# A fused attention and gated-unit kernel: output-row copies set apart, a later reciprocal, a third buffer for projected keys and queries

## The chip, the cores and the metric

The kernel runs on one core of one Trainium2 chip. The metric is the device time of one execution in microseconds (us); 814.01 us is the median of three runs of the kernel before (813.37 to 815.41). The profile is of one more execution, which took 813.36 us.

Names used below: PE is the matrix engine (TensorE), DVE the vector engine (VectorE), ACT the scalar engine (ScalarE), POOL is GpSimd. SP (SyncE) computes nothing here; it issues the DMAs, one after the other, in the order of the program. A DMA whose data is not there yet makes SP stand still, and every DMA behind it waits too.

## The reference

The input is x, 2048 rows of 640. It is normalised, goes through a 32-head attention (20 columns a head) and through a gated unit of width 1728, and the two results are multiplied and added to x:

```python
    def _A_ref(x, wqkv, wo):
        ...
        scores = jnp.einsum("bhqd,bhkd->bhqk", q, k) * scale
        p = _softmax(scores, axis=-1)
        o = jnp.einsum("bhqk,bhkd->bhqd", p, v)
        return (lambda x, *d: x.transpose(*d))(o, 0, 2, 1, 3).reshape(B, S, D) @ wo
    def _B_ref(x, w_gate, w_up, w_down):
        ...
        h = _sigmoid(g) * u
        return jnp.einsum("bsf,fd->bsd", h, w_down)
    xn = _layernorm(x, axis=-1)
    s = _A_ref(xn, A_wqkv, A_wo)
    g = _silu(_B_ref(xn, B_w_gate, B_w_up, B_w_down))
    return x + s * g
```

## The kernel before

**Blocks.** The attention is cut into 32 blocks (`NBLK`): eight groups of four heads times four chunks of 512 queries. Blocks 0 to 23 are six groups one after the other; in blocks 24 to 31 the last two groups alternate chunk by chunk (`gc_of`). A block has 64 jobs (`NJOB`): 16 tiles of 128 keys for each of its four heads. A job is a score matmul (line 883), an exponential, and a matmul with the values into the accumulator `oacc` (line 920). `oacc` holds 20 output rows and one row of sums for each of the four heads.

**Two ways to an exponential.** Most jobs go to ACT (line 82; two jobs of 512 columns in one instruction, `pt`, or one at a time, `px`). The others go to DVE: each score tile is converted to 16-bit integers (`iv`, line 1264), and then, for four jobs at a time, three passes (lines 998, 1001, 1004) make two halves of the exponential, which PE adds up by two matmuls.

**An order made at build time.** From line 1172 on the program steps through a clock of its own (`now`, in us) with a cost for each instruction, and writes PE's, ACT's and DVE's instructions in the order in which this clock lets them start. The engines then run these fixed orders and wait for each other through semaphores. Between attention work PE is given "items" (the projections, the gated unit, the output projection), chosen by position and by whether their inputs are due in the planner's clock. DMAs stand in SP's queue in the order in which the planner calls them.

**Normalising a block.** When the last value matmul of a block is out, `norm_a` copies `oacc` on DVE (`on`, line 949) and issues two DMAs: the rows of sums go to memory (`ld`, line 951) and come back spread over 128 partitions (`lt`, line 953). The pair `(time, block, on, lt)` is put in the list `timed`. Once that time has come, DVE runs `norm_b`: the reciprocal (`rt`, line 959), a DMA to memory (`rd`, line 961), four DMAs that bring it back broadcast to 32 rows each (`rl`, line 964); and four POOL products, each of 128 columns (`on_bf`, line 969), are put in `pool_q`, due 7.2 later. They leave `pool_q` in one of two ways:

- `beat` (line 933), after a DVE instruction that reads PSUM, emits one due product and makes it wait for the DVE instruction before that one, so that it runs beside the PSUM read;
- `flush("n")`, which `norm_a` and `norm_b` of the next block call first, emits whatever is left, with no such tie.

With the last product `norm_c` is called, which issues the copies of the block's 80 output rows to their place in `oU` (line 988): four or five DMAs, since a head whose rows cross a multiple of 128 takes two. `o_at[b]` says when the planner takes these rows as landed; the output projection of four row tiles (`mk_out`, line 778) waits for `o_at` of blocks 25, 27 and 29 (`need=ALT + 1 + 2 * (tt // 4)`). Block 31, the last, is normalised in another way, by transposes (`chain`, from line 1055), and the last four row tiles are projected at the end (`early`, `late_mm`, `tail_steps`). Block 30 is the last that goes through `norm_a` to `norm_c`.

**Projected keys and queries.** For the heads from 8 on, keys and queries are projected six heads at a time (`mk_ku`, `mk_qu`, line 536). DVE copies each 120 x 512 result out of PSUM into a tile with the tag `ku` (lines 547 and 586), SP writes it to memory (lines 548 and 587), and it is loaded later in the layout of the blocks (`kT`, `q`; lines 630 to 639). The rows of bounds (`bt`, line 606) take a tile of the same tag. There are two such tiles, so a copy waits until the DMA from the tile two before has been read out.

Of the kernel before, what the change touches and what calls it, by code (L numbers as in the profile page):

```python
# [11 lines left out]
BF16 = mybir.dt.bfloat16  # L12
# [6 lines left out]
P = 128  # L19
# [5 lines left out]
QC = 512  # L25
# [3 lines left out]
UC = UH * DH  # L29
# [22 lines left out]
def kernel(  # L52
# [11 lines left out]
    nc = tc.nc  # L64
# [27 lines left out]
    wk = ctx.enter_context(tc.tile_pool(name="wk", bufs=2))  # L92
# [8 lines left out]
    oU = persist.tile([P, KD, S], BF16, name="oU")  # L101
# [32 lines left out]
    def load_wv(pr):  # L134
        w = wk.tile([P, KD, 2 * GC], BF16, tag="wv", bufs=1, name="wv")
        nc.sync.dma_start(out=w, in_=wqkv_v[:, :, 2, pr * 2 * GC:(pr + 1) * 2 * GC])
        return w
# [306 lines left out]
    EL, PL = 0.15, 0.21  # L444
    T_F, T_PV, T_MM, T_MODE = 0.2133, 0.2133, 0.2133, 0.107
    T_IV, T_ON = 0.605, 0.60
    T_PASS = (0.1333, 0.1333, 0.27)

    def t_exp(n):
# [5 lines left out]
    def gc_of(b):  # L455
        if b < ALT:
            return divmod(b, NQC)
        return NG - 2 + (b - ALT) % 2, (b - ALT) // 2
# [80 lines left out]
    def mk_ku(u, c, at):  # L539
        st = {}  # L540

        def alloc():
            st["ps"] = misc_ps()

        def ev():
            st["k"] = wk.tile([P, QC], BF16, tag="ku", bufs=2, name="ku")[0:UC, :]
            ins = nc.vector.tensor_copy(out=st["k"], in_=st["ps"][0:UC, :])
            nc.sync.dma_start(out=kD[u][:, c * QC:(c + 1) * QC], in_=st["k"])
            return ins

        def mx():
            if u not in mku:
                mku[u] = [wk.tile([UC, NQC], FP32, tag="mk4", bufs=2, name="mk4"), 0, None]
            ins = nc.vector.tensor_reduce(out=mku[u][0][:, c:c + 1], in_=st["k"], axis=AXISX, op=ALU.max,
                                          apply_absolute_value=True)
            mku[u][1] += 1
            if mku[u][1] == NQC:
                mk = wk.tile([UC, 1], FP32, tag="mk", bufs=2, name="mk")
                nc.vector.tensor_reduce(out=mk, in_=mku[u][0], axis=AXISX, op=ALU.max)
                mku[u][2] = wk.tile([UC, UH], BF16, tag="mdu", bufs=2, name="mdu")  # L560
                ins = nc.vector.tensor_scalar_mul(out=mku[u][2], in0=esum_u[0:UC, :], scalar1=mk[:, 0:1])
            return ins

        def end(t):
            if mku[u][1] == NQC:
                ev_at[("mdu", u)] = t + 0.3
        return Item([("PE", alloc, [(T_MM, lambda kd=kd: u_mm(st, u, 1, c, kd)) for kd in range(KD)]),
                     ("DVE", 0.60, ev, "free", mark("kD", u, c)), ("DVE", 0.60, mx, "", end)], at,
                    pre=[("wu", u)])

    aqs = {}

    def mk_qu(u, c, at):
        st = {}

        def alloc():
            st["ps"] = misc_ps()

        def ab():
            aqs[(u, c)] = wk.tile([P, QC], BF16, tag="aq", bufs=4, name="aq")  # L580
            return nc.vector.tensor_scalar(out=aqs[(u, c)][0:UC, :].bitcast(I16), in0=st["q"].bitcast(I16), scalar1=0x7FFF,
                                           scalar2=0, op0=ALU.bitwise_and, op1=ALU.bitwise_or)

        def ev():
            st["q"] = wk.tile([P, QC], BF16, tag="ku", bufs=2, name="qu")[0:UC, :]
            ins = nc.vector.tensor_scalar_mul(out=st["q"], in0=st["ps"][0:UC, :], scalar1=qscale)  # L586
            nc.sync.dma_start(out=qD[u][:, c * QC:(c + 1) * QC], in_=st["q"])
            return ins
        return Item([("PE", alloc, [(T_MM, lambda kd=kd: u_mm(st, u, 0, c, kd)) for kd in range(KD)]),
                     ("DVE", 0.60, ev, "free", mark("qD", u, c)),  # L590
                     ("DVE", 0.19, ab, "", mark("aq", u, c))], at, pre=[("bD", u - 1)] if u else [])

    def mk_bu(u, at):
        st = {}

        def alloc():
            st["ps"] = misc_ps()

        def mm():
            for c in range(NQC):  # L600
                nc.tensor.matmul(st["ps"][32 * c:32 * c + UH, :], lhsT=mku[u][2], rhs=aqs[(u, c)][0:UC, :],
                                 start=True, stop=True, tile_position=(0, 32 * c), skip_group_check=True)

        def ev():
            bt = wk.tile([P, QC], BF16, tag="ku", bufs=2, name="bt")
            ins = nc.vector.tensor_copy(out=bt, in_=st["ps"])
            for c in range(NQC):
                nc.sync.dma_start(out=bD[u][:, c * QC:(c + 1) * QC], in_=bt[32 * c:32 * c + UH, :])
            return ins
        return Item([("PE", alloc, [(T_MM + 2 * T_MODE, mm)]),  # L610
                     ("DVE", 0.60, ev, "free", mark("bD", u))], at,
                    pre=[("mdu", u)] + [("aq", u, c) for c in range(NQC)])
# [333 lines left out]
    def norm_a(b):  # L946
        flush("n")
        on = w2.tile([P, QC], FP32, tag="on", bufs=2, name="on")
        beat(nc.vector.tensor_copy(out=on, in_=oacc))  # L949
        ld = dram.tile([GH, QC], FP32, name="ld", tag="ld")  # L950
        nc.sync.dma_start(out=ld, in_=on.rearrange("(j r) q -> j r q", r=32)[:, 0, :])
        lt = w2.tile([P, GH * QC // P], FP32, tag="lt", bufs=2, name="lt")
        nc.sync.dma_start(out=lt, in_=ld.rearrange("j (i c) -> (j i) c", c=GH * QC // P))
        return on, lt

    def norm_b(b, on, lt):
        flush("n")
        rt = w2.tile([P, GH * QC // P], FP32, tag="rt", bufs=2, name="rt")
        beat(nc.vector.reciprocal(out=rt, in_=lt), False)
        rd = dram.tile([GH, QC], FP32, name="rd", tag="rd")  # L960
        nc.sync.dma_start(out=rd.rearrange("j (i c) -> (j i) c", c=GH * QC // P), in_=rt)
        rl = w2.tile([P, QC], FP32, tag="rl", bufs=1, name="rl")
        for j in range(GH):
            nc.sync.dma_start(out=rl[32 * j:32 * j + 32, :], in_=rd[j:j + 1, :].broadcast_to((32, QC)))
        on_bf = w2.tile([P, QC], BF16, tag="on_bf", bufs=2, name="on_bf")

        def part(i):
            cs = slice(i * P, (i + 1) * P)
            ins = nc.gpsimd.tensor_tensor(out=on_bf[:, cs], in0=on[:, cs], in1=rl[:, cs], op=ALU.mult)  # L969
            if i == QC // P - 1:  # L970
                norm_c(b, on_bf)
                o_at[b] = now + 4.8
            return ins
        for i in range(QC // P):
            pool_q.append((now + 7.2, "n", lambda i=i: part(i)))

    def norm_c(b, on_bf):
        g, c = gc_of(b)
        for j in range(GH):
            f = g * GC + j * DH  # L980
            r = 32 * j + 1
            left = DH
            while left:
                t, o = divmod(f, P)
                m = min(left, P - o)
                if t == KD - 1:
                    o = f - FL if f >= FL else f - FK + D - FL
                nc.sync.dma_start(out=oU[o:o + m, t, c * QC:(c + 1) * QC], in_=on_bf[r:r + m, :])  # L988
                f += m
                r += m  # L990
                left -= m


    def passes(d, k):
# [109 lines left out]
    with tc.manual_schedule(engines={ENG.PE, ENG.Activation, ENG.DVE, ENG.Pool}):  # L1104
# [68 lines left out]
        while len(chain_end) < len(chain) or fill or items or glu_items or any(it.i < len(it.ops) for it in active):  # L1173
# [3 lines left out]
            if bb > blk_loaded:  # L1177
                blk_loaded = bb
                g, c = gc_of(bb)
                if c == 0 and g + 1 < PG:  # L1180
                    spread_wst(g + 1, load_wst(g + 1))
                if c == 0 and g + 1 < NG:
                    if g % 2 == 1:
                        wvs[(g + 1) // 2] = load_wv((g + 1) // 2)
            if not tail and all(ev_at.get(("h", NQC - 1, kf), 1e9) <= now for kf in range(NFT)):
                tail_load()
            active = [it for it in active if it.i < len(it.ops)]
# [18 lines left out]
            for eng in ("ACT", "DVE"):  # L1206
# [6 lines left out]
                if eng == "DVE" and norm_pending is not None and norm_pending[1] <= now and norm_pending[0] < NBLK - 1:  # L1213
                    free["DVE"] = now + T_ON
                    oacc_at[0] = now + T_ON + EL
                    timed.append((free["DVE"] + 6.5, norm_pending[0]) + norm_a(norm_pending[0]))
                    norm_pending = None
                    continue
                it = next((e for e in active if e.i < len(e.ops) and e.ops[e.i][0] == eng and e.open(now)), None)
# [5 lines left out]
                if eng == "ACT":  # L1225
# [24 lines left out]
                            s["ends"] = max(s["ends"], end + EL)  # L1250
                            nexp += 1
                    continue
                tm = next((x for x in timed if x[0] <= now), None)
                if tm is not None:
                    timed.remove(tm)
                    norm_b(*tm[1:])
# [173 lines left out]
            now += STEP  # L1430
        assert not items and not glu_items and not any(it.i < len(it.ops) for it in active)
        for tm in timed:
            norm_b(*tm[1:])
        flush("n", "o")
        tail_steps()

# [28 lines left out]
```

## Time and profile before

| | |
|---|---|
| median of three runs | 814.01 us (813.37 to 815.41) |
| profiled execution | 813.36 us |
| its span, first to last instruction | 811.6 us |
| granted TensorE clock | 0.995 |
| ACT: exponentials of two jobs (`pt`) | 697 of 1146 ns |
| DVE: `iv` / the three passes | 504 of 681 ns / 126 each of 685, 690 and 1221 ns |
| DVE: copy of `oacc` (949) / reciprocal (959) | 31 of 682 ns / 31 of 245 ns |
| POOL: product `on_bf` (969) | 124, median 456 ns, longest 1547 ns |
| SP: copies to `oU` (988) | 140, median 712 ns each to issue |

A line of a timeline has the start in us, the length in us, the engine and line, the operation, the tile written and read, and how often; in brackets stands the idle time of the engine before it and what ended that. The letter q behind an engine marks its instruction queue. A line of the waits has who waited, for whom, the total in us, how often, and the longest. DVE and ACT instructions overlap their neighbours a little, so that a row of `iv` starts every 0.60 us though one lasts 0.68.

### The profile page before, as it was taken

What the parts mean: (1) busy time and instruction counts of PE and PEld (TensorE: products, weight loads), DVE (VectorE), ACT (ScalarE), POOL (GpSimd) and SP (SyncE); (2) the same over time, 40 slices, a digit from 0 to 9 for tenths busy, and PEclk for the clock granted to TensorE, in tenths of its full rate; (3) what the DMA queues carried; (4) which work ended last, traced back from release to release, by engine and by line L of the source; (5) the groups of instructions that cost most, each with busy time, mean ns of one, the idle gap of its engine ahead of it and who ended that gap; (6) DMA issues with size and microseconds to landing.
All of it is one profiled execution on the core that took longest, in us unless ns stands there. A gap on an engine that the chain in (4) does not pass through costs nothing. (4 is left out here: it accounts for less than half of the span.)

```text
span 811.6 us, 17415 instructions
## 1 busy us (share of the span) xinstructions
PE 776.3 (96%) x6480; PEld 273.2 (34%) x6480; DVE 774.6 (95%) x1248; ACT 780.8 (96%) x991; POOL 107.7 (13%) x225
## 2 busy tenths in 40 slices
PE   7899999999999999999999999999999999999995
PEld 5522222333333323333333222333333223333332
DVE  7799999999999999999999999999999999999995
ACT  8899999999999999999999999999999999999991
POOL 7200000000010000000000000000100203203124
PEclk9999999999999999999999999999999999999998
DMA  5531211123222223212112131232222232312211
GB/s 160 156 103 50 66 52 40 59 58 96 63 70 69 68 58 85 66 55 61 55 58 67 51 100 54 71 104 81 63 70 60 72 88 67 123 57 82 83 52 61
DMA packets 91797, 59.96 MB, mean 74 GB/s; under 512 B 34868, under 2 KB 85604, under 8 KB 91712
## 3 DMA queue, kind: packets, MB, share of 16 engines
q1 hardware_dynamic: 91424, 58.52, 25.8%
q8 instruction: 51, 0.84, 0.4%
q14 instruction: 34, 0.28, 0.1%
q10 hardware_dynamic: 288, 0.33, 0.1%
HBM read 45.18 MB, written 11.09 MB: 69 GB/s over the span
## 5 line engine op out<-in xcount | busy, mean ns | idle before, releaser
L82 ACT ACTIVATE pt<-scA 128x1024 bf16<-128x1024 f32 x704 | 694.7, 1142 | 4.1 <-PE bk L883 3.1
L1264 DVE TENSOR_SCALAR iv<-bk 128x512 int16<-128x512 f32 x504 | 333.6, 681 | 10.2 <-PE bk L883 9.0
L883 PE MATMUL scA<-q,kT 32*128 32x512 bf16 x1401 | 273.1, 382 | 12.9 <-ACT pt L82 7.7
L883 PE MATMUL bk<-q,kT 32*128 32x512 bf16 x647 | 207.4, 383 | 0.1
L920 PE MATMUL oacc<-pt,v 128*21 128x512 bf16 x1401 | 179.4, 382 | 0.6 <-DVE on L949 0.6
L883 PEld LDWEIGHTS <-kT 32*128 32x128 bf16 x2048 | 84.1, 91 | 260.5 <-issue 249.6
L920 PE MATMUL oacc<-pb,v 128*21 128x512 bf16 x1008 | 159.7, 382 | 0.8 <-DVE pb L1004 0.7
L1004 DVE TENSOR_TENSOR pb<-iv,pb 128x2048 bf16<-128x2048 bf16 x126 | 153.9, 1221 | 1.0
L677 PE MATMUL bk<-xnT,wgu 128*128 128x512 bf16 x520 | 148.0, 383 | 1.6 <-DVE iv L1264 0.7
L969 POOL TENSOR_TENSOR on_bf<-on,rl 128x128 bf16<-128x128 f32 x124 | 59.3, 481 | 636.2 <-DVE pb L1004 160.1
L82 ACT ACTIVATE px<-bk 128x512 bf16<-128x512 f32 x143 | 100.5, 717 | 2.7 <-POOL hT L1113 1.6
L998 DVE TENSOR_SCALAR pb<-iv 128x2048 int16<-128x2048 int16 x126 | 86.3, 685 | 0.9
L1001 DVE TENSOR_SCALAR pb<-iv 128x2048 int16<-128x2048 int16 x126 | 86.9, 690 | 0.1
L723 PE MATMUL bk<-wd,hT 128*128 128x320 bf16 x448 | 83.8, 302 | 2.2 <-DVE iv L1264 1.4
L920 PEld LDWEIGHTS <-v 128*21 128x21 bf16 x2552 | 49.4, 91 | 86.4 <-issue 63.5
L677 PEld LDWEIGHTS <-wgu 128*128 128x128 bf16 x520 | 38.2, 97 | 67.6 <-issue 47.9
L920 PE MATMUL oacc<-px,v 128*21 128x512 bf16 x143 | 49.0, 382 | 0.0
L723 PEld LDWEIGHTS <-hT 128*128 128x128 bf16 x448 | 34.6, 97 | 41.4 <-issue 33.8
L536 PE MATMUL bk<-xnT,wu 128*128 128x512 bf16 x160 | 47.3, 383 | 1.2 <-DVE qu L586 1.0
L82 ACT ACTIVATE tnh<-bk 128x512 bf16<-128x512 f32 (+1 forms) x56 | 39.7, 709 | 0.1
L685 DVE SCALAR_TENSOR_TENSOR hT<-tnh,bk 128x512 bf16<-128x512 bf16 x52 | 35.3, 679 | 1.4 <-PE bk L677 0.7
L794 POOL TENSOR_TENSOR xnT<-otmp,xnT 128x160 bf16<-128x160 f32 x48 | 26.2, 567 | 47.9 <-DVE pb L1001 15.6
(111 smaller groups left out, 408.2 us busy)
## 6 DMA issues: line engine op xcount, KB each, us to landing
rl<-rd SPq DMA_DIRECT2D x124, 64.0 KB
wgu<-in_B_w_gate_dram SPq DMA_DIRECT2D x24, 320.0 KB
wgu<-in_B_w_up_dram SPq DMA_DIRECT2D x24, 320.0 KB
gq_dram<-gqs SPq DMA_DIRECT2D x24, 160.0 KB
xnT<-gq_dram SPq DMA_DIRECT2D x12, 320.0 KB
xt<-in_A_x_dram SPq DMA_DIRECT2D x16, 160.0 KB
xnT<-in_A_x_dram SPq DMA_DIRECT2D x16, 160.0 KB
out_dram<-xnT SPq DMA_DIRECT2D x14, 160.0 KB
```

What stands on the lines that cost most here:

```text
L82: return nc.scalar.add_instruction(mybir.InstActivation(func=func, name=nc.get_next_instruction_name(), engine=ENG.Activation, ins=[nc.sca ...
L536: nc.tensor.matmul(st["ps"], lhsT=wus[u][:, kd, i, :], rhs=xnT[:, c, kd, :], start=(kd == 0), stop=(kd == KD - 1))
L677: nc.tensor.matmul(st[key][0:fs, :], lhsT=w[:, i, kd, ko * P:ko * P + fs], rhs=xnT[:, c, kd, :], start=(kd == 0), stop=(kd == KD - 1))
L685: return nc.vector.scalar_tensor_tensor(out=hT[0:fs, kf, :], in0=st["t"][0:fs, :], scalar=1.0, in1=st["u"][0:fs, :], op0=ALU.add, op1=ALU. ...
L723: nc.tensor.matmul(st["ps"][:, 0:HD], lhsT=hT[:, kf, t4 * P:(t4 + 1) * P], rhs=wd[:, kf, h * HD:(h + 1) * HD], start=(kf == 0), stop=(kf = ...
L883: nc.tensor.matmul(dst, lhsT=kTs[gc_of(b)[0] % 2][32 * j:32 * j + 32, kt * P:(kt + 1) * P], rhs=qts[b % 3][32 * j:32 * j + 32, :], start=T ...
L920: nc.tensor.matmul(oacc[32 * j:32 * j + DH + 1, :], lhsT=lhsT, rhs=u["src"], start=first, stop=last, tile_position=(0, 32 * j), skip_group ...
L969: ins = nc.gpsimd.tensor_tensor(out=on_bf[:, cs], in0=on[:, cs], in1=rl[:, cs], op=ALU.mult)
L998: ins = nc.vector.tensor_scalar(out=pb[:, 0, :, :].bitcast(I16), in0=iv, scalar1=0x7F80, scalar2=1, op0=ALU.bitwise_and, op1=ALU.bitwise_or)
L1001: ins = nc.vector.tensor_scalar(out=pb[:, 1, :, :].bitcast(I16), in0=iv, scalar1=0x007F, scalar2=0x3F00, op0=ALU.bitwise_and, op1=ALU.bitw ...
L1004: ins = nc.vector.tensor_tensor(out=pb[:, 1, :, :], in0=iv.bitcast(BF16), in1=pb[:, 1, :, :], op=ALU.mult)
L1264: beat(nc.vector.tensor_scalar(out=d["iv"][:, j, :], in0=bank[bk], scalar1=B_OFF, scalar2=0.0, op0=ALU.add, op1=ALU.max))
```

## The change

Four things are changed:

- `norm_c` no longer issues a block's four or five `oU` copies in one go. For blocks 0 to 29 it puts them in `timed`, the first at once, the next each `T_OU` = 1.5 later; the main loop issues them as their time comes. `o_at[b]` grows by 1.5 for each copy after the first. Block 30 keeps the old way.
- The time after which DVE may run `norm_b` behind the copy of `oacc` is `T_LT` = 9.0 in place of 6.5, for blocks 0 to 29.
- The tag `ku` has three tiles in place of two.
- `timed` now holds two kinds of entries, told apart by their length; what is left of it at the end is run.

```diff
+    T_LT, T_OU = 9.0, 1.5
...
-            st["k"] = wk.tile([P, QC], BF16, tag="ku", bufs=2, name="ku")[0:UC, :]
+            st["k"] = wk.tile([P, QC], BF16, tag="ku", bufs=3, name="ku")[0:UC, :]
...
-            st["q"] = wk.tile([P, QC], BF16, tag="ku", bufs=2, name="qu")[0:UC, :]
+            st["q"] = wk.tile([P, QC], BF16, tag="ku", bufs=3, name="qu")[0:UC, :]
...
-            bt = wk.tile([P, QC], BF16, tag="ku", bufs=2, name="bt")
+            bt = wk.tile([P, QC], BF16, tag="ku", bufs=3, name="bt")
...
                 norm_c(b, on_bf)
-                o_at[b] = now + 4.8
...
     def norm_c(b, on_bf):
         g, c = gc_of(b)
+        parts = []
...
-                nc.sync.dma_start(out=oU[o:o + m, t, c * QC:(c + 1) * QC], in_=on_bf[r:r + m, :])
+                parts.append((oU[o:o + m, t, c * QC:(c + 1) * QC], on_bf[r:r + m, :]))
...
+        for i, (o, x) in enumerate(parts):
+            if b < NBLK - 2:
+                timed.append((now + T_OU * i, lambda o=o, x=x: nc.sync.dma_start(out=o, in_=x)))
+            else:
+                nc.sync.dma_start(out=o, in_=x)
+        o_at[b] = now + 4.8 + (T_OU * (len(parts) - 1) if b < NBLK - 2 else 0.0)
...
+            for tm in [x for x in timed if x[0] <= now and len(x) == 2]:
+                timed.remove(tm)
+                tm[1]()
...
-                    timed.append((free["DVE"] + 6.5, norm_pending[0]) + norm_a(norm_pending[0]))
+                    timed.append((free["DVE"] + (T_LT if norm_pending[0] < NBLK - 2 else 6.5), norm_pending[0]) + norm_a(norm_pending[0]))
...
-                tm = next((x for x in timed if x[0] <= now), None)
+                tm = next((x for x in timed if x[0] <= now and len(x) > 2), None)
...
         for tm in timed:
-            norm_b(*tm[1:])
+            tm[1]()
```

## The prediction

> **What bounds the kernel now.** I read first the busy times of the stretch from 31 to 793 us, the attention proper, then who waited in it, then the time line around each wait that the change touches, and last the end.
>
> ```profile
> 31.00:793.00 762.00, 742.90 (x6198) 250.84 (x6201) 741.54 (x1166) 756.74 (x941) 80.36 (x161) 1.00 0.26 73
> ACT pt L82 <- PE bk L883: 3.1, 7, 0.7
> ACT px L82 <- PE bk L883: 0.7, 1, 0.7
> DVE iv L1264 <- PE bk L883: 9.0, 18, 1.1
> DVE rt L959 <- DMA lt<-ld: 3.3, 4, 1.2
> DVE qu L586 <- DMA qD<-qu: 1.0, 1, 1.0
> ```
>
> The first line is one window: its length, then busy us of PE, weight loads, DVE, ACT and POOL, clock, DMA share and GB/s. ACT is busy 756.74 of 762.00 us: 5.3 us idle are the most that a better order at the same division of jobs could win here. DVE idles 20.5 us. The change aims at two DVE waits, 3.3 us in four places before the reciprocal and 1.0 us before one copy of queries. What ends them shows at the longest:
>
> ```profile
> 706.08 3.84 SPq L988 DMA_DIRECT2D oU<-on_bf  x5
> 709.97 0.53 SPq L951 DMA_DIRECT2D ld<-on  x1
> 710.60 2.08 SPq L1017 DMA_DIRECT2D xnT<-in_A_x_dram  x4
> 712.80 0.36 SPq L953 DMA_DIRECT2D lt<-ld  x1
> 714.99 0.25 DVE L959 RECIPROCAL rt<-lt 128x16 f32<-128x16 f32 x1 [1.23 <-DMA lt<-ld]
> 718.16 2.85 ACT L82 ACTIVATE pt<-scA 128x1024 bf16<-128x1024 f32 x3 [0.74 <-PE bk L883]
> ```
>
> The accumulator's copy starts at 706.03 and ends at 706.71, but SP is in the five `oU` copies of the block before until 709.92; the sums leave 3.3 us late, come back after DVE has arrived, and the hole of 1.23 us reaches ACT 3 us later as 0.74. The same picture, 3.0 to 3.8 us of `oU` copies ahead of `ld`, stands at the other three: holes of 0.74, 0.89 and 0.42 us on DVE at 235.73, 330.75 and 638.75, and on ACT 0.51 at 239.26, 0.42 at 336.07 and none. So 3.28 us of DVE's became **1.67 us of ACT's**. The wait of the queries at 444.72 has the same head (439.05, 3.53 us of copies, `qD` behind them at 442.68): 1.04 us on DVE, then on PE, then **0.74 us on ACT** at 446.48.
>
> **The change part by part.** No instruction is added or removed: 140 copies, 31 reciprocals, 124 products stay. Only orders move.
>
> *The copies.* Where the next block's `norm_a` flushes the last product, `norm_c` now only puts the copies on the list, and the loop finds them after `norm_a` has issued `ld` and `lt`. Elsewhere they stand 1.5 apart, so that `ld` meets one copy (0.71 us median), not 3.0 to 3.8. SP still stands at the first copy until POOL is done (58.2 us in 26 such waits, the longest 8.4), but no longer ahead of `ld` in the flushed blocks. Issue time on SP is the same in total, 140 x 0.71 = 99 us of 811.6, so nothing is lost there.
>
> *The reciprocal.* It now starts 2.5 later: 7.5 us (median of the 31) after the copy of `oacc` becomes about 10.1, the latest return seen is 8.95 (706.03 to 714.99). All four waits should go even without the copies' spreading. With it move one `rd` (0.34 us on SP), four `rl` (0.41 each) and four products. SP stands at `rd` until the reciprocal is there (65.7 us in 27, the longest 5.1); what queues behind it are loads of weights, keys and queries. PE's weight loads lost 0.4 us to `kT` in this stretch and nothing to `q`, so moving that stop costs nothing; if a load behind it became late, 5.1 us is the bound, once.
>
> *The third tile.* The copy at 444.72 would find a free tile. No instruction more. Either this or the spreading removes the 1.04.
>
> Gain on ACT: 1.67 + 0.74 = **2.4 us**. The upper bound is DVE's own 3.28 + 1.04 = 4.3, if DVE's time comes back whole; the lower is 0, if PE or the division of jobs eats it. I take 2.4, because ACT's row is the nearest to full.
>
> *What is late next, first: products.* In the 30 distances between accumulator copies (16.95 to 32.20 us, median 24), the four products now run from 15 to about 19 us after the copy. Added 2.5 by the planner's clock is 2.65 by the trace's (0.6 + 6.5 = 7.1 planned took 7.54). With each product moved so, 17 of them, in eight blocks, fall behind the next copy and are flushed without the tie to a PSUM read; today 3 do. An untied product can fall beside a DVE pass. What that costs is seen near the end, where POOL runs untied additions:
>
> ```profile
> 783.97 1.38 POOL L794 TENSOR_TENSOR xnT<-otmp,xnT 128x160 bf16<-128x160 f32 x3 [0.66 <-DVE rt L959]
> 784.88 1.01 DVE L1001 TENSOR_SCALAR pb<-iv 128x2048 int16<-128x2048 int16 x1
> ```
>
> The pass takes 1.01 where 0.68 is usual: 0.33 lost. Bounds: 0 (the product waits instead; one was stretched to 1.55) and 17 x 0.33 = 5.6 us of DVE. DVE's holes reached ACT at (1.67 + 0.74) / (3.28 + 1.04) = 0.56. I take a quarter of the products hitting a pass at its worst time: 4 x 0.33 x 0.56 = **0.7 us**. The Trainium skill speaks against this part: its page "SBUF — State Buffer", section "Who interferes with whom", says that GpSimd and DVE share a pair of ports under an exclusive lock, and that whoever starts first holds it for a whole instruction. The stretched pass above and the stretched product agree in kind; by that rule a pass could lose a whole product, and the sum would be the rival below.
>
> *Second: the output projection.* `o_at` of blocks 25, 27 and 29, four copies each, rises by 3 x 1.5 = 4.5 and by the later products. Before, the last product of block 29 runs at 774.48 and the first projection that needs it at 779.67, which is o_at's 4.8 in the trace's time: this is a real gate. After, the product is flushed at block 30's copy, 20.3 us after block 29's, near 776.0, and the gate opens (4.8 + 4.5) x 1.06 = 9.9 us later, near 786: 6.3 us late. For blocks 25 and 27 the gated unit's items fill the gap. For block 29 nothing is left (line 723 is last seen at 773.3):
>
> ```profile
> 776.86 0.39 PE L883 MATMUL scA<-q,kT 32*128 32x512 bf16 x2 [0.52 <-ACT pt L82]
> 779.18 0.39 PE L883 MATMUL scA<-q,kT 32*128 32x512 bf16 x2 [0.52 <-ACT pt L82]
> 779.67 0.84 PE L778 MATMUL bk<-wo,oU 128*128 128x320 bf16 x5
> 796.54 0.30 PE L778 MATMUL bk<-wo,oU 128*128 128x320 bf16 x1
> 798.54 0.39 PE L1025 MATMUL bk<-wo,oU 128*128 128x512 bf16 x1 [1.05 <-DMA oU<-on_bf]
> ```
>
> Without items PE idles: 0.36 (before 775.94) and twice 0.52, 1.4 us of the 3.7 from 775.94 to 779.67. In 6.3 us more that is 6.3 x 1.4 / 3.7 = 2.4 us of PE, to be paid back after the scores end at 793.5, where the chain to the end runs through PE. There, 1.05 us (798.54) and 0.68 (796.26) of PE's waits can take some of it. Bounds: 0, and the whole 6.3 us. I take 2.4 - 1.7 = **0.7 us**.
>
> The sum: -2.4 + 0.7 + 0.7 = -1.0 us. On the profiled execution's own 813.36 us (811.6 of span and 1.8 around it) that makes 812.4; the median stands 0.65 above that run, so I forecast **813.0 us** against 814.01. I take 0.3%, 2.4 us, as what a measurement here can tell from no change: under 811.6 is faster, over 816.5 slower.
>
> **The rivals.**
>
> *More comes back (faster).* DVE's 4.3 us come back whole and nothing is late: 814.0 - 4.3 = 809.7. And the planner deals the jobs anew, since each shifted reciprocal changes what it finds ready. A set of four more on DVE takes 4 x 573 ns = 2.3 us from ACT, for 4 x 0.60 + 2.6 = 5.0 us of DVE, which has that much: 807.4. Against it: ACT's idle of 5.3 caps the first way.
>
> *The last projection (slower).* Place: between block 29's products and the tail. If PE gives the eight projections no more room than now (779.67 to 796.84), they end 6.3 us later, and the 1.7 us of waits take nothing because they hang on block 30's copies: 814.0 - 2.4 + 6.3 = 817.9; with half the 2.4 us of gain, 819. It decides once the first projection comes more than the 2.4 us gained too late, after 782 (784 if the two waits do take their 1.7).
>
> *Products beside passes (slower).* All 17 at 0.33: 5.6 x 0.56 = 3.1, and 814.0 - 2.4 + 3.1 + 0.7 = 815.4; at a product's own 0.46 us, 17 x 0.46 x 0.56 = 4.4, so 816.7. For: eight short blocks. Against: a flushed product often ran free (the part may fall beside a PSUM read by chance). This is what the lock of the Trainium skill's page named above would do.
>
> *It does little.* If the later reciprocal alone had cured all, the copies' spreading would be idle; the time is the same as forecast, so no case of its own.
>
> **How the numbers follow.** Forecast, around 813.0 (811 to 815): 0.40, of which 0.06 falls under 811.6. More comes back: 0.34, all faster. Last projection: 0.16, slower. Products: 0.10, half of it slower. A new dealing of four jobs to ACT instead of DVE adds 2.3 us to any of these and takes 0.05 of the forecast's share to slower. That gives faster 0.40, the same 0.34, slower 0.26. The range must reach into both sides: down to 807.5 (the faster rival with one set), up to 818.0 (the projection's price); beyond are left 0.07 below and 0.1 above. The forecast's own range is 811 to 815.
>
> **What would show it.** Right: no wait of the reciprocal on `lt`, none of line 586 on `qD`; `oU` copies one at a time, with `ld` after at most one; ACT's idle from 31 us to the last exponential near 3 us; the first projection of the last group near 786. Wrong: the count of DVE jobs (504) moved by eight or more; new DVE waits on PE of over 3 us beyond the 9.0; passes above 0.9 us in more than ten places; or the stretch after the last exponential, 18 us now, changed by more than 2.

## The result, and the profile after

| | before | after |
|---|---|---|
| median of seven runs each (us) | 814.01 (812.82 to 816.15) | 811.31 (811.02 to 812.0) |
| profiled execution / its span | 813.36 / 811.6 | 811.31 / 809.3 |
| first exponential starts at | 30.30 | 29.97 |
| last exponential ends at | 793.50 | 789.15 |
| ACT idle between these two | 5.26 | 1.77 |
| from there to the end of the span | 18.15 | 20.19 |
| last projection of row tiles 8 to 11, behind the last exponential | 3.3 | 6.2 |

The ratio after to before is 0.9962, with a 95% interval of 0.9949 to 0.9975: faster by 0.38%; the medians lie 2.7 us apart. (Here and below the ratio is taken over all the runs, so it can differ by up to 0.1% from that of the two medians.) The runs also lie closer together, over 1.0 us in place of 3.3.

The stretch of the attention, one window of the kernel after (length, then busy us of PE, weight loads, DVE, ACT and POOL, clock, DMA share, GB/s):

```profile
31.00:789.00 758.00, 732.36 (x6115) 248.76 (x6178) 737.86 (x1159) 756.23 (x939) 78.58 (x157) 1.00 0.26 73
```

ACT now idles 1.8 of 758.00 us. Who waited there, in the kernel after (us in total, how often, the longest):

```profile
ACT pt L82 <- PE oacc L921: 0.9, 1, 0.9
ACT pt L82 <- PE bk L884: 0.2, 1, 0.2
DVE iv L1274 <- PE bk L884: 13.7, 25, 1.2
```

The rows `rt` on `lt` and line 587 (586 before) on `qD` are gone, and of ACT's eight waits on `bk` (3.8 us) one of 0.2 is left. What DVE lost there is in part lost elsewhere: its own wait for PE's scores, which stops nobody, grew from 9.0 to 13.7. DVE has 502 conversions in place of 504, and the same 126 of each pass (one of them now over half the columns): the division of jobs is as it was, give or take one pair.

But the copies do not stand as the change's spacing says. SP's part of the timeline of the kernel after, at the first block's copies and at a flushed block:

```profile
79.48 3.09 SPq L995 DMA_DIRECT2D oU<-on_bf  x4
...
560.88 2.34 SPq L995 DMA_DIRECT2D oU<-on_bf  x3
563.32 0.54 SPq L952 DMA_DIRECT2D ld<-on  x1
```

The first block's four go out back to back in 3.09 us (3.08 before). At 560.88 three copies still stand ahead of `ld`. Over the 31 blocks `ld` starts more than 2 us after the start of the copy of `oacc` in 14, against 10 before.

The end, in the timeline of the kernel after (PE, ACT, PE, DVE, PE, in order of time):

```profile
780.30 0.85 PE L779 MATMUL bk<-wo,oU 128*128 128x320 bf16 x5
...
786.08 3.08 ACT L82 ACTIVATE pt<-scA 128x1024 bf16<-128x1024 f32 x3
...
794.82 0.57 PE L779 MATMUL bk<-wo,oU 128*128 128x320 bf16 x3
...
796.11 0.32 DVE L754 TENSOR_TENSOR onq<-scA,rq 128x160 bf16<-128x160 f32 x1 [0.28 <-PE tp L1057]
...
796.80 0.39 PE L1032 MATMUL bk<-wo,oU 128*128 128x512 bf16 x1 [0.52 <-DMA oU<-on_bf]
```

The projections that need block 29 start at 780.30, 8.9 us before the last exponential ends; before it was 779.67 and 13.8 us. They end at 795.39, among the last block's own steps (`onq`, and the matmuls of line 1032).

### The profile page after: what moved, and what is told of

The parts are those of the page before. It is cut to its first block, busy times and chain, and to the rows that moved or that the text cites. A ratio compares the mean times of both kernels' runs of the same rounds, so it can differ in the third digit from the quotient of the medians.

```text
span 809.3 us, 17335 instructions
## 1 busy us (share of the span) xinstructions
PE 768.4 (95%) x6409; PEld 272.3 (34%) x6478; DVE 774.2 (96%) x1246; ACT 780.2 (96%) x989; POOL 109.1 (13%) x225
## 5 line engine op out<-in xcount | busy, mean ns | idle before, releaser
L1274 DVE TENSOR_SCALAR iv<-bk 128x512 int16<-128x512 f32 x502 | 333.0, 679 | 15.2 <-PE bk L884 13.7
L884 PE MATMUL bk<-q,kT 32*128 32x512 bf16 x642 | 201.1, 383 | 0.1
L678 PE MATMUL bk<-xnT,wgu 128*128 128x512 bf16 x476 | 141.8, 383 | 3.5 <-issue 1.3
L970 POOL TENSOR_TENSOR on_bf<-on,rl 128x128 bf16<-128x128 f32 x124 | 57.6, 471 | 629.0 <-DVE pb L1011 186.5
L537 PE MATMUL bk<-xnT,wu 128*128 128x512 bf16 x147 | 45.2, 383 | 1.4 <-issue 0.8
L795 POOL TENSOR_TENSOR xnT<-otmp,xnT 128x160 bf16<-128x160 f32 x48 | 29.9, 642 | 50.8 <-issue 28.0
```

What stands on the lines that cost most here:

```text
L537: nc.tensor.matmul(st["ps"], lhsT=wus[u][:, kd, i, :], rhs=xnT[:, c, kd, :], start=(kd == 0), stop=(kd == KD - 1))
L678: nc.tensor.matmul(st[key][0:fs, :], lhsT=w[:, i, kd, ko * P:ko * P + fs], rhs=xnT[:, c, kd, :], start=(kd == 0), stop=(kd == KD - 1))
L884: nc.tensor.matmul(dst, lhsT=kTs[gc_of(b)[0] % 2][32 * j:32 * j + 32, kt * P:(kt + 1) * P], rhs=qts[b % 3][32 * j:32 * j + 32, :], start=T ...
L1274: beat(nc.vector.tensor_scalar(out=d["iv"][:, j, :], in0=bank[bk], scalar1=B_OFF, scalar2=0.0, op0=ALU.add, op1=ALU.max))
```

## The experiments

The theory (A) was that the three kinds of wait are what the change wins. The rival (B) was that the new delays make the planner deal and order the jobs anew, and that this sets the time, for better or worse. So some kernels below keep PE's, ACT's and POOL's instructions in the order of before and move only DMAs or the reciprocal; others change the planner's numbers and let it deal. Kernels of one table were timed together.

| kernel | median (us) | ratio to before, 95% |
|---|---|---|
| before, with these | 814.25 | |
| `ku3_alone` | 813.35 | 0.9995, 0.9982 to 1.0007 |
| `copies_after_ld` | 811.46 | 0.9961, 0.9948 to 0.9974 |
| `recip_only` | 817.91 | 1.0037, 1.0022 to 1.0052 |
| `late_recip_alone` | 812.50 | 0.9977, 0.9966 to 0.9988 |

### The third tile alone

```diff
# ku3_alone, against before; in three places
-tag="ku", bufs=2
+tag="ku", bufs=3
```

> Only the third tile for projected keys and queries; every engine's order and SP's order are those of before. Theory A (removed waits come back as ACT's idle time): the 1.04 us wait of DVE at line 586 goes, ACT's idle from its first exponential to its last falls from 5.3 to about 4.5 us, and the time by 0.7 us (0.1%). Theory B (the gain is the planner's new dealing of the work): under 0.3 us, since no order changes.

The wait at the copy of queries is gone, ACT's idle is 4.75 us against 5.26, and the time is the same within its interval. The 0.74 us of ACT that the prediction put on this wait is of that size, and too small to time.

### The copies behind `ld`, orders of the engines kept

```diff
# copies_after_ld, against before
+    HOLD_OU = 2.0
...
-                nc.sync.dma_start(out=oU[...], in_=on_bf[r:r + m, :])
+                parts.append((oU[...], on_bf[r:r + m, :]))
...
+        for o, x in parts:
+            if b < NBLK - 2:
+                timed.append((now + HOLD_OU, lambda o=o, x=x: nc.sync.dma_start(out=o, in_=x)))
```

The main loop issues these entries as it does after the change; `o_at` stays. Only SP's order differs from before.

> Before with each block's oU copies issued 2.0 planner us later, all together; o_at as before, so PE, ACT, DVE and POOL keep their order and only SP's changes. Theory A with the copies' place as the cause: ld stands ahead of the copies in the flushed blocks, the four waits of the reciprocal (3.3 us) and the one of line 586 shrink to under 1 us in all, and the time falls by 1.5 to 2.4 us. Rival C (SP has no clock; where nothing flushes, the copies still come back to back ahead of ld): two or more of the four waits stay, and ld starts 2 us or more late in about as many blocks as before (11).

In the medians it wins as much as the whole change, 2.8 us. ACT's idle is 3.77 us, the wait at the copy of queries is gone, and of the reciprocal's four waits (3.28 us) three are left, 1.94 us in all. Why these are left shows in SP's part of its timeline, around the one that was longest before:

```profile
705.45 2.33 SPq L996 DMA_DIRECT2D oU<-on_bf  x3
707.89 0.52 SPq L952 DMA_DIRECT2D ld<-on  x1
708.46 1.51 SPq L996 DMA_DIRECT2D oU<-on_bf  x2
...
711.38 0.33 SPq L954 DMA_DIRECT2D lt<-ld  x1
```

Three copies still stand ahead of `ld` and two between `ld` and `lt`, so the wait fell from 1.23 us to 0.50 and did not go. At the other two that are left, three and four copies stand ahead of `ld`. Only around 325 us do all four stand behind it, and there the reciprocal's wait of 0.89 us is gone. So the signs of rival C came: three of the four waits stay, and `ld` starts more than 2 us after the start of the copy of `oacc` in 9 blocks, against 10. The time fell all the same. The profiled execution (812.02, the slowest of the five runs) shows 1.3 us of that against the first profile of before; where the rest of the medians' 2.8 us comes from, no profile shows.

### The later reciprocal alone, twice

```diff
# recip_only, against before
+    LATE_B, late_b, due_b = 1.6, [], {}
...
-                    norm_b(*tm[1:])
+                    due_b[tm[1]] = now + 7.2
+                    if tm[1] < NBLK - 2:
+                        late_b.append((now + LATE_B, tm[1:]))
+                    else:
+                        norm_b(*tm[1:])
                     free["DVE"] = now + 0.16
...
+                if eng == "DVE" and late_b and late_b[0][0] <= now:
+                    norm_b(*late_b.pop(0)[1])
...
-            pool_q.append((now + 7.2, "n", lambda i=i: part(i)))
+            pool_q.append((due_b[b], "n", lambda i=i: part(i)))
# late_recip_alone, against before
-timed.append((free["DVE"] + 6.5, ...
+timed.append((free["DVE"] + (9.0 if norm_pending[0] < NBLK - 2 else 6.5), ...
```

In `recip_only` the planner charges and deals as before; 30 reciprocals stand two or three instructions further on in DVE's order, and their `rd` and `rl` further on in SP's. `late_recip_alone` is the change's own edit of the time, dealt anew.

> Before's planner and its orders on PE, ACT and POOL untouched; only the reciprocals of blocks 0 to 29 stand 1.6 planner us further on in DVE's own order, the products due as before. Theory A: all four waits of the reciprocal go, ACT's idle falls by 1.7 us to about 3.6, the time by 1.7 us (0.2%), the stretch after the last exponential stays at 18.1 us. Theory B: the waits go but ACT's idle and the time move by less than 0.5 us.

> Before with 9.0 in place of 6.5 and nothing else, so the planner deals anew, with o_at later only by the products. Theory A: waits of the reciprocal gone, gain 1.7 us or more on ACT, the last group's projection about 3 us late instead of 6, the stretch after the last exponential under 1 us longer: 812 to 812.5. Theory B: anything from 808 to 816, with ACT's idle not tied to the waits (2.9 us in before) moving by over 1 us.

`recip_only` was slower than before, by 0.37%, which neither theory expected. Its waits of DVE and ACT between 31 and 793 us:

```profile
DVE qu L587 <- DMA qD<-qu: 3.2, 1, 3.2
DVE rt L960 <- DMA lt<-ld: 0.5, 1, 0.5
ACT pt L82 <- PE bk L884: 4.7, 5, 3.6
```

The reciprocal's waits shrank to 0.5 us, and one at the queries' copy grew from 1.04 to 3.2, of which ACT lost 3.6 in one piece. How, is in SP's part of the timelines. First before, then `recip_only`:

```profile
428.38 0.34 SPq L961 DMA_DIRECT2D rd<-rt  x1
...
430.40 1.69 SPq L964 DMA_DIRECT2D rl<-rd  x4
```

```profile
428.92 0.34 SPq L962 DMA_DIRECT2D rd<-rt  x1
...
433.90 0.35 SPq L639 DMA_DIRECT2D q<-qD  x1
434.36 1.71 SPq L965 DMA_DIRECT2D rl<-rd  x4
...
440.17 3.51 SPq L989 DMA_DIRECT2D oU<-on_bf  x5
443.78 0.89 SPq L588 DMA_DIRECT2D qD<-qu  x2
```

`rd` is only 0.5 us later, but `rl` now stands behind the loads of `q`, which wait for PE, and goes out 4.0 us later. With it come the products, then the five copies (439.05 before, 440.17 now) and `qD` behind them (442.68, now 443.78). DVE arrives 1.07 us sooner at the copy of queries (442.61 in place of 443.68), since it had waited less before. So 1.04 + 1.10 + 1.07 = 3.21. The profiled execution (815.14) is one of the fastest of the twelve (815.02 to 820.41); what makes the median 2.8 us longer still, no profile shows.

`late_recip_alone`, with the same delay but jobs dealt anew, was faster than before by 0.23%: its waits at the tag `ku` (0.57 and 1.21 us) fell elsewhere, ACT's idle is 3.61 us, and the stretch after the last exponential is 17.95. The two lie 5.4 us apart. That can be read for B, but what `recip_only` lost is a wait, as the next table shows.

### Parts together, and the last block's gate

| kernel | median (us) | ratio to before, 95% |
|---|---|---|
| before, with these | 813.75 | |
| `recip_and_ku3` | 810.52 | 0.9957, 0.9941 to 0.9974 |
| `all_held` | 810.51 | 0.9953, 0.9932 to 0.9974 |
| `gate29_as_before` | 815.30 | 1.0010, 0.9996 to 1.0023 |
| `apart_without_later` | 810.88 | 0.9961, 0.9948 to 0.9973 |

```diff
# recip_and_ku3: recip_only with three tiles
# all_held: copies_after_ld + recip_only with three tiles
# gate29_as_before, against after; in three places
-NBLK - 2
+NBLK - 3
# apart_without_later, against after
-    T_LT, T_OU = 9.0, 1.5
+    T_LT, T_OU = 6.5, 1.5
```

> The kernel of recip_only with three tiles for projected keys and queries; all engines' orders and SP's order are those of recip_only. Theory A2 (SP's stop at the later rd holds up the qD copies behind it, and with two tiles DVE pays for that): the wait of 3.2 us at line 587 goes, ACT's idle falls from 7.5 to about 3.4 us, and the time lies some 4 us under recip_only, 2 to 2.5 us under before. Rival (the later reciprocal costs in itself): over before's time.

> Before's planner and orders on PE, ACT and POOL; the reciprocals 1.6 further on, three tiles, and the copies 2.0 later in SP's queue. Theory A: no wait of the reciprocal or of lines 547 and 587 is left, ACT's idle is 2.9 us (before's 5.3 without the 2.4 tied to the waits), the time 2.4 us under before's profile, and runs spread over about 1 us as in after. Theory B (after gained by the new dealing): under 1 us. After less than copies_after_ld's 0.39% gain would mean that the waits of the reciprocal matter little beside the copies' place.

> After with block 29 treated like block 30 (reciprocal at 6.5, copies at once, o_at as before), blocks 0 to 28 as in after. Theory: the stretch after the last exponential, 20.2 us in after and 18.2 in before, is longer because the last group's projection opens late; it falls back to 18 to 18.5 and the time by 1.5 to 2 us, to about 809.5. Rival: the tail's length comes from how the last jobs fall (two jobs fewer on DVE), and the time stays within 0.7 us of after's 811.3 or rises.

> After with 6.5 in place of 9.0: copies apart, o_at raised, three tiles; orders as in before up to about 690 us. Theory A with the copies' place as the cause: as copies_after_ld up to there (two to three short waits of the reciprocal, 1 to 2 us in all, none at line 587), ACT's idle near 3.5, then a tail 0.5 to 2 us longer from the raised gate: 811.5 to 813. Rival (only the later reciprocal removes the waits): four waits of 3 us or more stay and the time is 814 or more.

**`recip_and_ku3`** shows what made `recip_only` slow: the two differ by the third tile alone. SP and DVE in its timeline:

```profile
441.17 3.51 SPq L989 DMA_DIRECT2D oU<-on_bf  x5
...
443.53 0.68 DVE L587 TENSOR_SCALAR qu<-bk 120x512 bf16<-120x512 f32 x1
...
444.78 0.89 SPq L588 DMA_DIRECT2D qD<-qu  x2
```

The copies and `qD` are as late as there, and DVE's copy runs at 443.53 without a wait. A tile that alone gave nothing is worth 817.91 - 810.52, some 7 us, once the reciprocal is later (across two tables; the medians of before in them are 0.5 apart). The two profiled executions lie 3.3 us apart (815.14 and 811.85).

**`all_held`** has all three cures and no wait of DVE on a DMA. ACT's idle is 3.19 us, and the waits of ACT that remain in it are small ones on PE:

```profile
ACT pt L82 <- PE bk L885: 1.1, 4, 0.3
ACT px L82 <- PE bk L885: 0.6, 1, 0.6
ACT pt L82 <- PE scA L885: 0.5, 2, 0.3
```

Its median is that of `recip_and_ku3`: once the reciprocal is later and the tile is there, the place of the copies adds nothing that shows. Its runs spread over 2.3 us, not over about 1 as was expected.

**`gate29_as_before`** takes block 29 out of the change. The last projections did come back, to 3.7 us after the last exponential (6.2 after the change), but the kernel got slower and not faster, so the expectation failed. The timeline of its end:

```profile
799.07 0.33 DVE L754 TENSOR_TENSOR onq<-scA,rq 128x160 bf16<-128x160 f32 x1 [3.45 <-DMA oU<-on_bf]
```

The last block's second scaled tile `onq` shares its two buffers with `on_bf`, and here it waits for block 30's five `oU` copies, which still read one. Those were issued from 793.86 to 797.64, and `onq` starts at 799.07. In the kernel after, the same instruction (796.11, shown above) waits for PE's transposes of the first `onq` alone; what makes it wait for the copies here is not shown. So this run does not isolate the last projections: with their return came another wait of 3.45 us.

**`apart_without_later`** is the change with the old time of the reciprocal. It still has three waits of the reciprocal (2.8 us together), so the copies' spacing does not remove them; and it is no slower than the change. Its stretch after the last exponential is 17.24 us, 0.9 shorter than before, though `o_at` is raised as in the change; a longer one was expected.

### Other times for the reciprocal, and the best of the parts

| kernel | median (us) | ratio to before, 95% |
|---|---|---|
| before, with these | 814.13 | |
| `apart_and_recip` | 808.55 | 0.9926, 0.9913 to 0.9938 |
| `later_8` (`T_LT` 8.0) | 812.60 | 0.9975, 0.9963 to 0.9987 |
| `later_10` (`T_LT` 10.0) | 814.93 | 1.0008, 0.9998 to 1.0018 |

`apart_and_recip` is `apart_without_later` with the reciprocal set back as in `recip_only` (`LATE_B` = 1.6), so that the planner deals as with 6.5 while DVE runs the reciprocal later. Beside these three, the kernel before was profiled once more.

> The kernel of apart_without_later with the reciprocals of blocks 0 to 29 standing 1.6 planner us further on in DVE's order, products due as there; PE, ACT and POOL keep their order. Theory A: its three waits of the reciprocal (2.9 us on DVE) go, ACT's idle falls from 3.5 to about 2.2, and the time by 1 to 1.5 us to 809.5, the fastest so far. Rival (what was won came from the copies' place and the third tile, the reciprocal's waits being covered by now): within 0.5 us of 810.9.

> After with the reciprocal 8.0 behind the copy of oacc in place of 9.0; the planner deals anew. If the waits are all there is, they are gone here too (the return needs 8.3 us at most), ACT's idle is under 2.5 us and the time 811 within 1 us. If the dealing decides, the tail and the time differ by 2 us or more although no wait is left.

> After with 10.0 in place of 9.0. As for later_8: no waits left, and 811 within 1 us if waits are all there is; 2 us or more away, with the difference in the stretch after the last exponential or in ACT's idle on PE, if the dealing decides.

> The kernel before once more, for a second profile. Its runs spread from 812.8 to 818.4 where after's lie within 1 us. If the spread comes from the waits on SP's queue, the waits of lines 959 and 586 and ACT's idle differ from the first profile's 4.3 and 5.3 us by about as much as the times do; if not, they agree within 0.3 us and the spread lies elsewhere.

**`apart_and_recip`** beats both kernels, by 5.6 us the one before. Its only ACT waits between the first and the last exponential are these of its table:

```profile
ACT pt L82 <- PE bk L885: 0.9, 3, 0.3
```

ACT's idle is 1.92 us, the stretch after the last exponential 17.24, and DVE has no wait on a DMA.

**`later_8` and `later_10`** have at most one wait of the reciprocal left (1.20 us and none), and yet their medians and the change's are 812.60, 814.93 and 811.31. So it is not these waits that set that spread of 3.6 us, but what the new dealing moved. Against the span of the kernel after, `later_8` has 1.5 us more of ACT's idle (3.31, where under 2.5 was expected), 1.3 more of its busy time, a start 0.9 later and an end 2.1 shorter. `later_10` has 1.7 more of ACT's busy time and an end 1.6 longer, and in that end the wait of `onq` on block 30's copies is back, 3.47 us.

**`before_again`**: a second profile of the kernel before (814.34 us, span 812.6) has longer waits than the first. Its waits of DVE on DMAs:

```profile
DVE rt L959 <- DMA lt<-ld: 4.1, 4, 1.5
DVE qu L586 <- DMA qD<-qu: 1.8, 1, 1.8
```

They make 5.9 us, against 4.3 in the execution that the prediction was made from, and ACT's idle is 6.62 against 5.26.

## Why the prediction came out as it did

The forecast was a little faster, 813.0; it came to 811.31, inside the forecast's own range just past the 811.6 from which a gain can be told, and with a gain of 2.7 us where the sum gave 1.0. The direction was right, and so was its main reason; three steps behind it were not, and two of the signs that were to speak against it did appear. That the total came near is in part luck. In the profiled spans ACT's side gave 4.0 us where the sum had 1.7 (2.4 less 0.7), and the end cost 2.0 where it had 0.7, so two errors took from each other.

Of the theories both hold. With PE's, ACT's and POOL's orders kept, `recip_and_ku3` and `all_held` win as much as the change, so removed waits alone are worth that (A). Among kernels with at most one wait of the reciprocal left, a new dealing moves the time by 3.6 us (B).

- **The gain term, 2.4 us of ACT's idle: mechanism right, mis-sized.** `all_held`, where the waits go and PE, ACT and POOL keep their orders, lowers ACT's idle from 5.26 to 3.19, 2.07 us: the term is right for the execution it was read from. But that was a mild one. The second profile has 1.6 us more of the waits and 1.36 us more of ACT's idle, and `all_held` lies 3.2 us under before in the medians (0.47% by the ratio). The prediction added the 0.65 us between the first profiled run and the median to the forecast as if it were constant. If the waits' varying length is in it, it goes away with them; that is argued from two profiles of before, 1.0 us apart in span, and not shown.
- **The rest of ACT's gain goes with the new order.** After the change ACT idles 3.5 us less than before, 1.4 more than the waits explain. `all_held` has the waits cured with the old order; the change has a new one. That the order counts is shown by the three values of `T_LT`; which of its moves won the 1.4 is not.
- **"So that `ld` meets one copy": wrong.** SP keeps no time. The 1.5 us are distances in the planner's clock and fix nothing but the order of issue; where SP stands at the first copy until POOL is done, all that follow go out behind each other, as at 79.48. What frees the reciprocal is its own place: after the change it runs 9.3 to 10.8 us after the copy of `oacc`, behind the return of even late sums, whereas `apart_without_later` keeps the copies' spacing and three of the waits.
- **"So moving that stop costs nothing": wrong.** The prediction asked what queues behind `rd` and `rl`, and not what these would queue behind in their new place. `recip_only` shows it: `rl` behind loads that wait for PE, 4.0 us late, and the price at a tile's reuse 11 us on. SP stands 75.6 us at `rd` there, and 88.1 after the change, where 65.7 were read before. The row of SP's waits in the kernel after:

```profile
SPq L962 <- DVE rt L960: 88.1, 25, 7.9
```

  The longest such stop, 7.9, is beyond the bound of 5.1 that the prediction gave. The change has no such wait, and it also has the third tile. That tile was costed as one of two cures for the same 1.04 us; with the order of before, it is what makes the later reciprocal safe (`recip_and_ku3`). No run takes it out of the change itself.
- **Products beside passes: right in DVE's time, in part by luck.** Forecast 4 x 0.33 = 1.3 us of DVE; passes are stretched by 1.85 us in sum before (10 of them) and by 3.09 after (16), so 1.24 more, and no stretch is longer than 0.33. But that sum holds what ran beside POOL's additions of the projected rows too: beside products it is 0.59 us (4 passes) before and 1.39 (8) after, 0.80 more. And 10 products in five blocks fall behind the next copy of `oacc`, not 17 in eight. The Trainium skill, page "SBUF — State Buffer", section "Who interferes with whom", would have a pass lose up to a whole product; these rows show less, and the rival built on it did not come. What of the 1.24 reached ACT can't be told apart from the new order.
- **The last projection: late as forecast, but mis-sized, and its way to the end was another.** The gate opened 9.0 us after block 30's copy of `oacc` (771.29 to 780.30; forecast 9.9), and measured against the last exponential the first projection is 5.0 later than before (forecast 6.3). The prediction let two waits of 1.7 us take most of the 2.4 us of lost PE time and kept 0.7. The stretch after the last exponential grew by 2.0. The larger of the two waits hangs on block 30's copies, and these moved too. POOL and SP in the timeline of the kernel after, then SP before:

```profile
789.48 3.72 POOL L795 TENSOR_TENSOR xnT<-otmp,xnT 128x160 bf16<-128x160 f32 x4
793.17 0.87 POOL L970 TENSOR_TENSOR on_bf<-on,rl 128x128 bf16<-128x128 f32 x2
794.06 3.78 SPq L997 DMA_DIRECT2D oU<-on_bf  x5
```

```profile
795.77 3.79 SPq L988 DMA_DIRECT2D oU<-on_bf  x5
```

  POOL adds the projected rows to the output. After the change four such additions, 3.72 us in all, stand between block 30's second product and its last two, so its copies start 4.9 us after the last exponential, against 2.3 before. PE's matmuls of the last four row tiles wait for them in both kernels (796.80 and 798.54), 7.65 and 5.04 us after the last exponential, and the chain of work that ended last runs through these copies in both. In the other kernels:

| kernel | last projection ends, after the last exponential | block 30's copies start, after it | to the end of the span | less the wait of `onq` |
|---|---|---|---|---|
| `apart_and_recip` | 3.3 | 1.5 | 17.24 | 17.2 |
| `apart_without_later` | 3.3 | 1.5 | 17.24 | 17.2 |
| `late_recip_alone` | 3.3 | 1.9 | 17.95 | 18.0 |
| before | 3.3 | 2.3 | 18.15 | 18.2 |
| `later_10` | 3.6 | 1.5 | 21.77 | 18.3 |
| `gate29_as_before` | 3.7 | 1.9 | 21.73 | 18.3 |
| `later_8` | 4.3 | 1.3 | 18.07 | 18.1 |
| after | 6.2 | 4.9 | 20.19 | 20.2 |

  Only the kernel after has the projections and these copies late, and only its end is long once the wait of `onq` is taken off. The raised `o_at` without the later reciprocal (`apart_without_later`) and the later reciprocal without the raised `o_at` (`late_recip_alone`) do not lengthen the end. This is an argument from eight profiles, in which other things differ too; no run isolates it, since the one meant to brought the wait of `onq` with it. That wait stands nowhere in the prediction.
- **The rivals.** The first, more comes back, is nearest in its sign: DVE's waits went whole, and the idle of ACT fell by more than they explain. It did not reach its 809.7; the tail took 2.0 back. The extra set of jobs did not come (126 passes of each kind, as before). The second, the last projection, did come late, and the end grew by a third of its price (2.0 of 6.3).
- **The signs.** Seen as written: no wait on `lt` or `qD`, 502 conversions. Not seen: copies one at a time; the first projection near 786 (it came at 780.30, since block 30's copy of `oacc` was 4.7 us earlier); ACT's idle near 3 us (1.77). Seen against: DVE's waits on PE up by 4.7 (over 3 was to be a bad sign) and the last stretch up by 2.04 (over 2). The first of the two was a poor sign: ACT did not wait for it.

In the profiled spans the account is: ACT's idle -3.5, its busy time -0.5, the start -0.3, the end +2.0, together -2.3 us (811.6 to 809.3).

What stays open: what makes the DMA waits of the kernel before longer in some executions than in others; whether these waits are the part of the medians' gains that the profiles do not show; which move of the planner won the 1.4 us; and how much of the longer end is due to the late projections.

## What to carry to other kernels

A queue's order made at build time is not a schedule: spacing DMAs in a planner's clock only decides who stands behind whom, so when one that waits is moved, look both at what is now behind it and at what it is now behind. Remove a wait by giving slack at its end (a later use, one more buffer) and test such parts together, since here a third tile alone gave nothing and the later reciprocal alone lost 0.37%, and the pair won 0.43%. Before sizing a wait on a DMA, profile twice: one execution can show it a quarter too short.

## What was not expected of the hardware

Waits on DMA round trips differ between executions of one and the same kernel: 4.3 and 5.9 us in two profiles of the kernel before. Whether they make the spread of the times is not shown. The seven runs after lie within 1.0 us and the five of `apart_and_recip` within 0.8 (808.01 to 808.83), where the seven before spread over 3.3; but `all_held`, with no wait of DVE on a DMA up to the last exponential, spreads over 2.3.
